# A D-skip by loads and VectorE products in place of diagonal matmuls, with a new instruction order

## The chip, the cores and the metric

The kernel runs on one core of a Trainium2 chip. The metric is the device time of an execution in microseconds (us). A profile covers one execution and gives its span, 1.7 to 2.2 us less than the timed figure in most executions, up to 3.7 us in some. Where a run was timed in rounds, it alternated with the kernel before on the same chip. Executions carry a state: one that is over 1.5% above the fastest of the same kernel counts as slow, and ratios use fast ones only. The trace also gives the clock granted to TensorE, as a share of full speed (1.00 in the profile before).

## The reference, cut to what matters

Two layers side by side, 640 channels each, on a sequence of 2048.

```python
# layer A: a diagonal complex state space layer
for t in range(L):
    h = Lam_bar * h + Bu[:, t, :]
y = 2.0 * einsum("blp,dp->bld", hseq, Cmat).real + x * Dskip   # x * Dskip is the "D-skip"
# layer B: a short shift convolution, a long FFT convolution, and a gate
kv = (k shifted by 0..3, weighted) * v
out_b = q * (longconv(kv, ssm_k) + kv * ssm_D)
```

The change concerns only the last term of layer A. Both layers share the engines all the time.

## The kernel before: the parts that matter

The kernel doesn't leave its order to a scheduler. A long text, `ORDER`, lists about 750 named operations. Each engine executes its own operations in the order of that text, and a suffix says where an operation with a choice goes (`/A` ScalarE, `/D` VectorE, `/G` GpSimd, `/S` SyncE's queue) and which buffer it gets (`@2`).

The names that the argument needs: `dn` are the up-projections of layer A, `m1` a first combination with rotation tables M, `S0` and `S5` the coarse sums over the sequence, `d0`/`a0` and `d1`/`a1` the way back (a matmul, then an addition on VectorE), `py` the output projection in 16 tiles of two halves, `ey` the tile's eviction and `st` its store. `set_4_0` and the like are halves of the tables M (M_4, first five channel groups). `s1`, `s2`, `i2`, `i1` are the stages of layer B's long convolution, `cv`, `cs`, `ca`, `cm` its shift convolution, `kz` a memset of the pad columns of k, `kvl` a reload through DRAM.

The output projection before, with the D-skip as matmuls against blocks of diag(D):

```python
for j in range(10):
    nc.tensor.matmul(P[:, part, 0:320], lhsT=hap(j), rhs=self.CT[:, j, c0:c0 + 320],
                     start=(j == 0), stop=False)
...                                               # pieces: the 2 or 3 blocks of 128 channels in this half
for q, (k, lo, hi) in enumerate(pieces):
    nc.tensor.matmul(P[:, part, lo - c0:hi - c0], lhsT=self.xT[...], rhs=self.diagD[:, k, ...],
                     start=False, stop=(q == len(pieces) - 1))
...
self.evac(f"ey_{r}{i}", 640, ...)                 # a copy on ScalarE or VectorE
```

A table half is one product of two SBUF operands, on either engine:

```python
self.eng[e].tensor_tensor(out=mt[:, js, :]..., in0=E[:]...to_broadcast(...), in1=sap()[:, js, :]...to_broadcast(...), op=ALU.mult)
```

Of the kernel before, what the change touches and what calls it, by code (L numbers as in the profile page):

```python
# [9 lines left out]
ALU = mybir.AluOpType  # L10
# [10 lines left out]
D = 640  # L21
# [125 lines left out]
ld_lre kz2/D@0 w0 xn0@0 scol pidx Dm0 B00 consts J0 w1 E0 kz1/G@1 ci0@1 w2 zero J1 c4 wi1@2 ld_lim ld_ldt xn1@2 wi0@3 bc  # L147
px00@0 B01 px02@1 wm1 nrow ex00/A ex02/A par@2 px04@3 p0 nrowf dtb Dm1/S wm0 B10 px10@0 ex04/A px12@1 E1 px14@2 p1 ex12/A nrho
x121 fi mk rn ph ci1 ld_sk/S dn0_2_0@4 x130 ex10/D trig dn0_0_0@6 B11 ex14/D ws1@4 R dn1_2_0 rc ss dn1_1_0@0 set_3_0/D
set_2_0/G dn1_0_0 e1_2_0/A dn1_4_0@2 set_1_0/D ws0@5 k0@6 kz0/G set_1_1/G x131 dn0_4_0 e1_0_0/D hst0/S@2 m1_2_0 x120 set_3_1/G  # L150
dn0_1_0 e3_2_0/D e1_4_0/D m1_0_0 dn1_8_0@4 ct@3 set_2_1/G e3_0_0/D e1_1_0/D dn0_8_0 sk x101 cv300/D@4 dn1_9_0@6 set_4_1/D
m1_1_0 dn0_9_0 cs200/D@3 v0@5 e1_8_0/A dtap0/D set_8_1/D m1_4_0 e3_1_0/A m1_8_0 e3_4_0/A ca200 s1h03@0,4 x100 e3_8_0/A s1h01@2
e1h03/A dn0_3_0@4 cs100/D x111 e1h01/A ca100 s1h00@0 x110 e1_9_0/A s1h02@2 cs000/D dn1_3_0 kz3/G@2 e1h00/A ca000 hst1/S@6
m1_9_0 e1h02/A dn1_7_0@0 cm00 e1_3_0/A s2h02@2,5 den kvs0/S dn0_7_0 e3_9_0/A k1 e2h02/A set_12_0/D s2h03@6 m1_3_0 g e2h03/A
dn0_4_1@2 e1_7_0/A s2h01@6 dn1_4_1 e2h01/A dtap1/D set_G_0/G set_8_0/D m1_7_0 e3_3_0/A kvl0/S@3 s1h10@6,0 e3_7_0/A k2 s1h12@4
e1h10/A set_G_1/D dn0_0_1@0 set_12_1/G e1h12/A s1h11@6 set_4_0/D dn1_0_1 e1_4_1/A ld_dsk/G e1h11/A m1_4_1 cv310/D@5 s1h13@4
e3_4_1/A cs210/D@4 v1@6 s1k03@6,2 e1h13/A dn0_1_1@2 ca210 e1k03/A s1k00@4 cs110/D e1_0_1/A s1k02@6 V dn1_1_1 e1k00/D e1k02/A
m1_0_1 ca110 e1_1_1/A s2h00@4 s1k01@6 e3_0_1/A cs010/D m1_1_1 e1k01/A dn1_3_1@0 cv320/D@3 e3_1_1/A ca010 s2k03@6,1 e2h00/A
dn0_3_1 cm10 e2k03/A s2k01@2,4 s2k00@4 e2k01/A kvs1/S dn1_2_1@6 e2k00/D k3 e1_3_1/A s2k02@2 pP00@6 s2h11@4,1 e2k02/A dn0_2_1
pQ00 e2h11/A m1_3_1 cn00@3 dn0_8_1@2 e3_3_1/A pP01@5 e1_2_1/A s2h12@4 s2h13@0 pY00 e2h12/A dn1_8_1 e2h13/A m1_2_1 pQ01  # L160
kvl1/S@4 i200@4,4 e3_2_1/A i201@0 e300/A pY01 S0@6 v2@6 e301/A dn1_9_1@4 cs220/D@1 eS0/A ca220 i202@0 e1_8_1/A i203@6 cn10
dn0_9_1 cs120/D e302/A ca120 e303/A s1k10@0,2 m1_8_1 cs020/D e1_9_1/A zt0@5 dn1_6_1@6 e3_8_1/D e1k10/A ca020 m1_9_1 s1k11@2
e3_9_1/A s1k13@0 cm20 e1k11/A s1k12@4 dn0_6_1 e1k13/A e1k12/D jw0@2 e1_6_1/A s2h10@0 q0/S@5 jsw0 dn0_7_1@4 cn11@0 e2h10/A Ct
jcw0 jaw00 scan0 hst2/S@0 s2k13@2,1 s2k12@0 e2k13/A dn1_7_1 e2k12/A dn1_5_0@2 e1_7_1/A s2k11@0,4 pP11@6 cn01 dn0_5_0 e2k11/A
pQ11 m1_7_1 s2k10@0 e3_7_1/A m1_6_1 e2k10/A pY11 dn1_6_0@4 e1_5_0/A i100@0 pP10@1 kvs2/S e3_6_1/A dn0_6_0 dtap2/G ob00 m1_5_0
s1h22@6,4 e3_5_0/A pQ10 e1_6_0/A s1h20@0 dn1_5_1@2 e1h22/A pY10 dn0_5_1 e1h20/A kz4/G@3 k4 diagD hst3/S@4 jv0@6 e1_5_1/A
i213@0,2 jsv0 m1_6_0 e313/A m1_5_1 i211@6 e3_5_1/D e3_6_0/A i212@0 jcv0 e311/A i210@2 kvl2/S@6 jav00 S5@4 v3@1 jav01 e312/A
e310/D d1_0@6 eS5/A ct00@0 a1_0 ct01@2 ect00/A jw5@4 jcw5 s1h23@6 ect01/A dtap3/D jsw5 ct10@0 e1h23/A ct11@2 jaw50 i101@4
scan5 ect11/A ct20@6 ect10/A s1h21@2 ect20/A s1k23@0,1 q1/S@0 ob01 e1h21/A d1_2@6 d1_3@7 a1_2 jv5@4 ob0/S e1k23/A ct21@2 zt1@5
jsv5 ect21/A ct30@0 jcv5 s1k21@4 jav51 ect30/A s1k22@2 jav50 d1_4@6 e1k21/A a1_3 d1_9@0 d1_5@1 a1_4 e1k22/A d1_7@7 a1_9 d1_6@6  # L170
ct31@4 a1_5 ct40@2 ect31/A d1_1@0 a1_6 d1_8@1 a1_7 ect40/A ct41@4 d00_6@6 a1_8 ect41/A d00_7@7 d00_0@2 a1_1 d00_5@3 cs230/A@5
d00_2@1 d00_8@0 a00_5 py0_32@4,0 a00_6 a00_2 py1_32 a00_7 a00_8 s1k20@6 ey_32/A a00_0 d00_9@3 d00_4@1 e1k20/A st_32/S d00_3@0
a00_9 d00_1@2 i111@4 a00_1 cv330/A@6 a00_3 i110@6 a00_4 s1h33@2,0 ca230 py0_03@0,1 e1h33/A ob11 cs130/A py1_03 ob10 py0_33@2,0
ey_03/A ca130 st_03/S ob1/S py1_33 cs030/D ca030 d01_1@4 s1h32@6 ey_33/A a01_1 s1h30@0 st_33/S e1h32/A cm30 d01_9@5 hst4/S@2
d01_3@4 py0_02@2,1 cv340/A@5 cs240/D@1 kvs3/S a01_9 py1_02 e1h30/A ca240 d01_0@5 py0_00@6,0 ey_02/D cs140/A a01_0 st_02/S
dtap4/G s2h20@0,3 a01_3 d01_8@5 s2k21@2,0 e2h20/A a01_8 d01_6@4 py1_00 kvl3/S@6 ca140 e2k21/A a01_6 s2k20@0 ey_00/A d01_5@5
d01_2@4 e2k20/A d02_6@2 st_00/G a01_5 s2h21@6 d01_4@3 a02_6 d01_7@5 e2h21/A py0_31@0,1 a01_7 cs040/A a01_2 s1k33@6,2 a01_4
s1k30@4 s1k32@2 pP20@3 e1k30/A py1_31 e1k32/A ca040 py0_12@4,0 e1k33/A pQ20 q4/S@1 ey_31/A py1_12 pY20 st_31/S d02_5@2 s2h23@6
v4@0 ey_12/A a02_5 d02_3@3 s2h22@0 e2h23/A a02_3 d02_1@2 d02_7@4 d02_2@5 a02_1 e2h22/A s1k31@6 st_12/S a02_2 d02_9@3 e1k31/A
s1h31@0 a02_9 d02_4@2 a02_7 d02_8@5 e1h31/A s2k22@6,6 d02_0@3 a02_8 e2k22/A i220@0,5 a02_4 i221@4 a02_0 e320/A s2h33@6,4 cm40  # L180
s2h30@2 py0_21@0,1 e2h30/A e2h33/D kvs4/S e321/A py1_21 s2k23@2 ey_21/A s2h32@6 e2k23/D st_21/S s1h40@4,1 e2h32/A s1h42@0
kvl4/S@4 pP21@3 s2k31@2,0 e1h42/A py0_20@6,0 e2k31/D e1h40/A s2k32@0,5 pQ21 s2k33@4 e2k32/A s2h31@2 py1_20 pY21 e2k33/A pP31@6
py0_22@0,1 ey_20/A e2h31/A st_20/S pQ31 s1h41@4 s1k40@6,0 pY31 s1h43@2 e1k40/A py1_22 q2/S@2 e1h41/D e1h43/A s2k30@6 ey_22/D
s2h41@2,3 e2k30/A i223@4 st_22/G e2h41/D s1k41@0 e323/A s1k42@6 pP30@5 py0_13@2,0 e1k42/A pQ30 e1k41/A py1_13 pY30 s1k43@4
i222@6 ey_13/D e1k43/A i231@0,2 e322/D st_13/S i232@2 e331/A s2k40@4,4 e332/D s2k41@6 zt2@4 e2k40/A s2h42@0 e2h42/D e2k41/A
s2h40@2 i230@4 e2h40/A i233@6 e330/D py0_30@0,1 e333/A pP40@0 s2h43@2 s2k42@4,3 pQ40 zt3@1 e2h43/A s2k43@6 py1_30 pY40 e2k42/A
e2k43/A py0_23@2,0 ey_30/A pP41@5 i121@4 pQ41 st_30/S q3/S@6 i240@6,0 i241@0 pY41 e340/A py1_23 e341/A i242@6 ey_23/A i243@0
e342/A st_23/G i120@2 e343/D py0_10@6,1 ob20 zt4@5 ob21 i131@0 i130@2 ob31 py1_10 ob30 ob2/S py0_11@4,0 ey_10/D st_10/S ob3/S
py1_11 i140@0 ey_11/A st_11/G i141@2 ob40 py0_01@6,1 ob41 py1_01 ob4/S ey_01/A st_01/S
# [3 lines left out]
class Kernel:  # L193
# [65 lines left out]
    def setup(self):  # L259
# [14 lines left out]


# [24 lines left out]
        Et = T([128, 64], i32, "Et")  # L300

        op("E0", {"POOL": 0.2}, lambda e: g.iota(Et[:], pattern=[[1, 64]], base=128, channel_multiplier=-1), w=["Et"])

        def f_E1():
            v.tensor_single_scalar(out=Et[:], in_=Et[:], scalar=63, op=ALU.bitwise_and)
            v.tensor_single_scalar(out=E[:], in_=Et[:], scalar=0, op=ALU.is_equal)
        small("E1", f_E1, ["Et"], ["E", "Et"], 0.4)
        J = T([128, 128], bf16, "J")
        Jt = T([128, 128], i32, "Jt")
        ident = T([128, 128], bf16, "ident")  # L310
        self.J, self.ident = J, ident
        op("J0", {"POOL": 0.3}, lambda e: g.iota(Jt[:], pattern=[[1, 128]], base=64, channel_multiplier=-1), w=["Jt"])

        def f_J1():
            v.tensor_single_scalar(out=ident[:], in_=Jt[:], scalar=64, op=ALU.is_equal)
            v.tensor_single_scalar(out=Jt[:], in_=Jt[:], scalar=127, op=ALU.bitwise_and)
            v.tensor_single_scalar(out=J[:], in_=Jt[:], scalar=0, op=ALU.is_equal)
        small("J1", f_J1, ["Jt"], ["J", "ident", "Jt"], 1.0)
# [7 lines left out]
        def f_nrow():  # L326
            g.iota(nrow[:, 0:3, :], pattern=[[1, 3], [0, 10]], base=1, channel_multiplier=0)
            g.iota(nrow[:, 3:7, :], pattern=[[4, 4], [0, 10]], base=4, channel_multiplier=0)
        small("nrow", f_nrow, [], ["nrow"], 0.3, "POOL")
        small("nrowf", lambda: v.tensor_copy(out=nrowf[:], in_=nrow[:]), ["nrow"], ["nrowf"], 0.5)  # L330

        lpar = T([128, 3, 10], f32, "lpar")
        lre, lim = lpar[:, 1, :], lpar[:, 2, :]
# [102 lines left out]
        def f_bc():  # L436
# [3 lines left out]
            v.tensor_scalar(out=offc[:], in0=ptmp[:], scalar1=-2048.0, scalar2=4096.0, op0=ALU.mult, op1=ALU.add)  # L440
        small("bc", f_bc, ["pidx"], ["bcol"], 0.6)

        ws = T([128, 96], i32, "ws")
        rowa = T([128, 2], f32, "rowa")
        colw = T([128, 1], f32, "colw")
        pr = T([128, 2], i32, "pr")
# [728 lines left out]
```

## Time and profile before

| | before |
|---|---|
| median of 3 runs | 202.42 us (200.48 to 203.70) |
| profiled span, clock | 200.5 us, 1.00 |
| TensorE busy | 185.7 us, 93% |
| VectorE, ScalarE, GpSimd busy | 168.1, 148.1, 20.6 us |
| first up-projection matmul | 11.93 us |
| first coarse sum S0 | 61.33 to 62.47 us |
| first output projection | 104.6 us |
| last inverse unit (i140) | 191.48 us |

The four marks at the bottom are start times of TensorE's groups in the timeline.

### The profile page before, as it was taken

The page shows a single profiled execution, that of the slowest core. Times are in us where ns is not written, and L with a number is a line of the kernel's source. Part 1 is how long each engine was busy: PE and PEld are TensorE (multiplying, and loading weights), DVE is VectorE, ACT ScalarE, POOL GpSimd, SP SyncE. Part 2 cuts the span into 40 slices and gives each one's busy share as a digit, 9 for nine tenths or more (in the row PEclk, how much of TensorE's full clock was granted, in tenths as well). Part 3 has the DMA queues.
Part 4 walks back from the last instruction along what each step waited for, and adds up shares of the span by engine and source line. Part 5 has one row for each costly group of instructions (what it writes and reads, how often), then busy time and mean ns, then how long its engine had stood idle before and what let it go on. Part 6 is the DMA issues. An engine that isn't in the chain of part 4 may idle for free.

```text
span 200.5 us, 8859 instructions
## 1 busy us (share of the span) xinstructions
PE 185.7 (93%) x4043; PEld 136.3 (68%) x4043; DVE 168.1 (84%) x264; ACT 148.1 (74%) x175; POOL 20.6 (10%) x35
## 2 busy tenths in 40 slices
PE   0599999979999999699999999999999999999982
PEld 0465566747777678467657777676787878788771
DVE  7899899876899999949988899788959999877540
ACT  4979998978899888389986749896967679752011
POOL 8056500700000000000000000100000010001010
PEclk9999999999999999999999999999999999999999
DMA  5999997999999999969995068509334334998985
GB/s 167 239 152 132 231 180 167 245 159 210 219 180 171 167 217 206 247 153 215 210 196 133 5 152 252 134 22 189 89 147 103 96 80 105 170 234 160 229 226 140
DMA packets 109959, 33.74 MB, mean 168 GB/s; under 512 B 107106, under 2 KB 108642, under 8 KB 109922
## 3 DMA queue, kind: packets, MB, share of 16 engines
q1 hardware_dynamic: 109668, 32.52, 83.9%
q8 instruction: 31, 0.51, 1.1%
q0 software_dynamic: 224, 0.66, 0.9%
q14 instruction: 6, 0.05, 0.1%
q10 hardware_dynamic: 30, 0.00, 0.0%
HBM read 9.19 MB, written 7.86 MB: 85 GB/s over the span
## 4 chain that ended last, share of the span: by engine, by line
PE 72%; DMA 14%; DVE 6%; ACT 3%; SPq 2%; issue 1%; POOL 0%; DVEq 0%; POOLq 0%; ACTq 0%
PE ps L806 20%; PE ps L658 17%; PE ps L909 9%; PE ps L945 8%; PE ps L231 4%; DMA s<-s 4%; PE ps L1001 4%; DMA s<-in_B_v_dram 4%; PE ps L233 4%; PE ps L1037 3%; DMA s<-in_A_x_dram 3%; DMA s<-in_B_ssm_k_dram 3%; DVE s L239 2%; PE ps L810 2%; ACT s L237 2%
## 5 line engine op out<-in xcount | busy, mean ns | idle before, releaser
L237 ACT CAST s<-ps 128x1024 bf16<-128x1024 f32 x86 | 84.1, 1018 | 16.9 <-PE ps L945 6.4
L658 PE MATMUL ps<-xT,BC 128*64 128x512 bf16 x400 | 49.1, 383 | 0.1
L806 PE MATMUL ps<-BC,hb 128*128 128x320 bf16 x240 | 36.4, 300 | 0.0
L658 PEld LDWEIGHTS <-BC 128*64 128x64 bf16 x400 | 22.3, 110 | 15.1 <-issue 0.9
L806 PEld LDWEIGHTS <-hb 128*128 128x128 bf16 x240 | 21.9, 98 | 8.7 <-issue 0.3
L968 DVE TENSOR_TENSOR s<-s,s 128x2048 bf16<-128x2048 bf16 x20 | 24.4, 1222 | 2.0 <-ACT s L237 0.7
L909 PE MATMUL ps<-R,s 64*64 64x128 bf16 x1280 | 22.5, 218 | 2.9 <-POOL s L831 1.8
L237 ACT CAST yo<-ps 128x640 bf16<-128x640 f32 x12 | 8.4, 698 | 22.7 <-PE ps L810 18.5
L909 PEld LDWEIGHTS <-s 64*64 64x64 bf16 x1280 | 18.7, 107 | 8.1 <-issue 3.7
L239 DVE CAST s<-ps 128x1024 bf16<-128x1024 f32 x14 | 17.0, 1220 | 8.3 <-PE ps L909 2.7
L945 PE MATMUL ps<-s,Wre 128*64 128x128 bf16 x320 | 21.4, 221 | 0.0
L763 DVE TENSOR_TENSOR hb<-ps,hb 128x512 bf16<-128x512 f32 x30 | 19.1, 684 | 2.8 <-PE ps L231 1.6
L945 PE MATMUL ps<-s,Wim 128*64 128x128 bf16 x320 | 21.2, 219 | 0.0
L945 PEld LDWEIGHTS <-Wre 128*64 128x64 bf16 x320 | 18.2, 110 | 2.5 <-issue 0.5
L884 DVE TENSOR_TENSOR s<-s,s 128x2048 bf16<-128x2048 bf16 x15 | 18.3, 1222 | 1.0 <-ACT s L876 0.7
L945 PEld LDWEIGHTS <-Wim 128*64 128x64 bf16 x320 | 18.1, 110 | 1.1
L1044 DVE TENSOR_TENSOR s<-ps,s 128x1024 bf16<-128x1024 f32 x10 | 11.8, 1216 | 4.1 <-PE ps L1037 3.9
L237 ACT CAST hb<-ps 128x768 bf16<-128x768 f32 x17 | 13.7, 808 | 1.1 <-PE ps L658 1.1
L968 DVE TENSOR_TENSOR s<-s 128x1024 bf16<-128x1024 bf16 x20 | 13.8, 688 | 0.3
L231 PE MATMUL ps<-hb,M 128*64 128x256 bf16 (+1 forms) x136 | 13.3, 296 | 0.0
L1037 PE MATMUL ps<-Ct,s 128*64 128x64 bf16 x640 | 11.6, 196 | 0.8 <-DMA s<-s 0.7
L1037 PEld LDWEIGHTS <-s 128*64 128x64 bf16 x640 | 11.1, 113 | 1.9 <-DMA s<-s 0.9
(157 smaller groups left out, 261.4 us busy)
## 6 DMA issues: line engine op xcount, KB each, us to landing
s<-in_B_ssm_k_dram SPq DMA_DIRECT2D x5, 512.0 KB, 4.7
kvd<-s SPq DMA_DIRECT2D x5, 512.0 KB, 4.4
s<-kvd SPq DMA_DIRECT2D x5, 512.0 KB, 5.6
s<-in_B_q_dram SPq DMA_DIRECT2D x5, 512.0 KB, 4.4
out_dram<-s SPq DMA_DIRECT2D x5, 512.0 KB, 5.1
out_dram<-yo SPq DMA_DIRECT2D x12, 160.0 KB, 2.8
s<-in_A_x_dram SPq DMA_DIRECT2D x2, 640.0 KB, 4.8
out_dram<-yo POOLq DMA_DIRECT2D x4, 160.0 KB, 3.4
```

Of the source, the lines that this page charges most:

```text
L231: self.nc.tensor.matmul(out[h], lhsT=lhsT[:, h], rhs=rhs, **k)
L237: self.nc.scalar.copy(out=out, in_=in_)
L239: self.eng[e].tensor_copy(out=out, in_=in_)
L658: nc.tensor.matmul(P[64 * ri:64 * ri + 64, b, :], lhsT=self.BT[:, k, ri, 64 * j:64 * j + 64], rhs=self.xT[:, k, hf, 2 * b:2 * b + 2, :].re ...
L763: v.tensor_tensor(out=hv(r), in0=self.P(p2)[:, 0, :].rearrange("p (h m) -> p h m", h=2), in1=hv(r), op=ALU.add)
L806: nc.tensor.matmul(P[:, part, 0:320], lhsT=hap(j), rhs=self.CT[:, j, c0:c0 + 320], start=(j == 0), stop=False)
L884: op(f"ca{j}{G}{h}", {"DVE": dve_tt(W_)}, lambda e, c=c, tt=tt: v.tensor_tensor(out=c(), in0=c(), in1=tt(), op=ALU.add), r=[f"tm{G}{h}"], ...
L909: nc.tensor.matmul(P[64 * ri:64 * ri + 64, r, 128 * b4:128 * b4 + 128], lhsT=d[64 * r:64 * r + 64, 4 * qd + b4, a0, :], rhs=self.R[64 * r: ...
L945: nc.tensor.matmul(P[64 * pi:64 * pi + 64, ri, 128 * k4:128 * k4 + 128], lhsT=W[:, kp, pi, :], rhs=A[:, kp + 16 * pi, :], start=True, stop ...
L968: v.tensor_tensor(out=o, in0=a, in1=b, op=op_)
L1037: nc.tensor.matmul(P[64 * ah:64 * ah + 64, b // 8, 64 * (b % 8):64 * (b % 8) + 64], lhsT=Z[:, 16 * h + b, 64 * ri:64 * ri + 64], rhs=self. ...
L1044: v.tensor_tensor(out=o, in0=self.P(pt)[:].rearrange("p s (b a c) -> p a (s b) c", b=8, a=16), in1=o, op=ALU.mult)
```

## The change

The intent is to take 96 small matmuls off TensorE, which is the bound. Each output tile now loads its rows of x again, VectorE multiplies them by D, and the eviction from PSUM becomes an addition. Memory for it is won by letting small buffers share space. B is loaded in three pieces, eight matmuls on zeros run on TensorE as a warm-up, and the whole `ORDER` was searched anew under the assumption that GpSimd and VectorE hold each other up (in the profile before, two table halves that take 1.25 and 0.81 us alone take 1.92 and 1.87 side by side). The code part, cut:

```diff
-                    nc.tensor.matmul(P[:, part, 0:320], ..., start=(j == 0), stop=False)
-                pieces = [...]
-                for q, (k, lo, hi) in enumerate(pieces):
-                    nc.tensor.matmul(P[:, part, lo - c0:hi - c0], lhsT=self.xT[...], rhs=self.diagD[...], start=False, ...)
+                    nc.tensor.matmul(P[:, part, 0:320], ..., start=(j == 0), stop=(j == 9))
-        self.evac(f"ey_{r}{i}", 640, ...)
+        op(f"xl_{r}{i}", ... dma_start(out=self.yo[yo.slot][:], in_=self.x2[r0:r0 + 2033:16, :]) ...)
+        op(f"xm_{r}{i}", ... nc.vector.tensor_tensor(out=yo, in0=yo, in1=self.Db[:], op=ALU.mult) ...)
+        op(f"ey_{r}{i}", ... nc.vector.tensor_tensor(out=yo, in0=self.P(pt)[:, :, 0:320], in1=yo, op=ALU.add) ...)
+        op("warm", {"PE": 1.9}, f_warm, ...)          # eight matmuls on zeros
-        self.yo = [... for i in range(2)]
+        self.yo = [... for i in range(4)]
```

Of the order, one stretch, as the changed kernel has it for GpSimd's queue (other engines' words cut):

```
... kz4/G kz3/G set_4_1/G set_12_0/G set_8_1/G set_12_1/G set_4_0/G set_G_0/G xl_03/G@2 set_8_0/G set_G_1/G xl_02/G@3 ld_dsk/G ... S0
```

Before, GpSimd made six table halves, all by 39 us. VectorE made the other eight.

## The prediction

> **What bounds the kernel now.** I read the page's shares first, then the busy time in stretches, then the chain that ended last, then the idle time of each group, and last the timelines of GpSimd and VectorE around the rotation tables M.
>
> ```profile
> span 200.5 us, 8859 instructions
> PE 185.7 (93%) x4043; PEld 136.3 (68%) x4043; DVE 168.1 (84%) x264; ACT 148.1 (74%) x175; POOL 20.6 (10%) x35
> ...
> 0.00:12.00 12.00, 4.98 (x45) 4.24 (x47) 10.17 (x44) 7.75 (x11) 5.44 (x19) 1.00 0.89 189
> 12.00:42.00 30.00, 30.00 (x520) 18.41 (x522) 27.88 (x54) 28.38 (x38) 12.20 (x10) 1.00 1.06 191
> 42.00:62.00 20.00, 18.89 (x458) 13.90 (x454) 15.98 (x16) 16.57 (x23) 0.00 (x0) 1.00 1.18 188
> 62.00:105.00 43.00, 40.96 (x947) 28.63 (x942) 38.34 (x67) 35.37 (x47) 0.52 (x2) 1.00 1.09 199
> 105.00:191.00 86.00, 85.59 (x1935) 66.74 (x1932) 73.33 (x84) 58.77 (x60) 1.91 (x4) 1.00 0.61 136
> 191.00:200.50 9.50, 5.32 (x154) 4.34 (x154) 2.35 (x2) 1.23 (x2) 0.54 (x1) 1.00 0.72 181
> ```
>
> TensorE is the bound. From 12 to 191 us (columns after the two lengths: TensorE, weight loads, VectorE, ScalarE, GpSimd) it is idle only 1.1 + 2.0 + 0.4 us; the rest of its idle time is the start and the tail. VectorE has about 13 us left between 105 and 191 us. So a microsecond off the matmul stream is a microsecond off the span, and so, reversed, is any new hole in it.
>
> ```profile
> 104.77 1.36 PE ps L806 x10
> 106.13 0.14 PE ps L810 x3
> 106.27 1.36 PE ps L806 x10
> 107.63 0.14 PE ps L810 x3
> ```
>
> This is the chain in the output projection. Each half tile is ten matmuls, 1.36 us, then three against diag(D), 0.14 us.
>
> ```profile
> 9.68 2.31 PE ps L607 x20
> 11.99 8.10 PE ps L658 x35
> ...
> 36.11 1.25 POOL L422 TENSOR_TENSOR M_G<-E,sg 128x640 bf16<-128x640 bf16 x1 [6.34 <-DVE sg L405]
> 37.32 1.92 POOL L422 TENSOR_TENSOR M<-E,ss 128x640 bf16<-128x640 bf16 x1
> ...
> 37.32 0.81 DVE L422 TENSOR_TENSOR M<-E,ss 128x640 bf16<-128x640 bf16 x1
> 38.05 1.87 DVE L422 TENSOR_TENSOR M_G<-E,sg 128x640 bf16<-128x640 bf16 x1
> ```
>
> One table half takes 1.25 us on GpSimd and 0.81 on VectorE alone; where both want one at once, 1.92 and 1.87. All of GpSimd's tables are done by 39.2 us here, more than 20 us before the first coarse sum reads them (61.3 us).
>
> [...] the first 20 transposes of 128 columns take 2.31 us, 116 ns each. [...] the trace has 0.49 and 0.81 us for 640 elements.
>
> **The change, part by part.**
> Removed from TensorE: 6 matmuls in each of 16 tiles, 32 groups x 0.14 = 4.5 us, all in the stream that sets the end, so -4.5 us.
> Added at the start: 8 matmuls of 512 columns on zeros before the second half of x has landed (TensorE waits for it anyway)[...] But the second x load is now issued behind four transposed loads of B where it stood behind one, so I book -0.7 us.
> Moved: the tile eviction goes wholly to VectorE as an addition from PSUM (16 x 0.82 where it had 4, +9.8 us) with a product before it (16 x 0.49 = +7.8). In return VectorE loses 4 evictions of 1024 (-4.9), 2 of 768 (-1.9), 2 table halves, 2 scalings (-1.5), diagD (-1.1), and gains 3 copies of xT (+1.8). With the rows of the page VectorE comes to about 176 us. From the first projection to the last inverse unit (i140) I sum 80 us for it against 78 for TensorE; consecutive VectorE spans overlap by some 0.08 us in the trace, so the real occupancy is lower, and it just fits. I book +0.5 us.
> Loads: 16 x 160 KB are 2.6 MB more on 33.7 MB, mostly when the DMA share is 0.61, far ahead of use: 0.
> Shorter buffers, B in three pieces: 0.
>
> The new order is what I trust least. The semaphores of the built program show one thing plainly. GpSimd's queue is in order, and in it the two small memsets of the pad columns of k for groups 4 and 3 now stand ahead of all eight table halves. The first waits for VectorE's scaling cs120, the second for a matmul of i202 (inverse of group 0), because those buffers are still being read. The first coarse sum on TensorE (S0) waits for the M_4 and M_8 halves, and the seventh of the eight is the one it needs; an x load issued by GpSimd stands among them. So S0 can't start before i202 + about 0.3 + 7 x 1.25 + 0.5 for the load's issue = i202 + 9.6 us with nobody in the way[...]. Between i202 and S0 TensorE has only i203 0.5, one L658 group 1.1, three s1 units 1.5, two of L231 0.66: with i202 itself 4.2 us. All its later work waits behind S0. Before, i202 ran at 63.65 us; the order puts 1.2 us less of matmuls ahead of it, so it comes near 61.5. S0 would be reached near 65.5 and start near 72: a hole of 5 to 9 us, taken as 7. [...]
>
> Sum for the span: 200.5 - 4.5 - 0.7 + 0.5 + 7 + 0.8 = 203.6 us; some later small waits (1.8 us at 82 us, for a load that goes through GpSimd) may dissolve in the hole, -0.9: 202.7. The timed figure stood 1.9 us above the profiled span (202.42 against 200.5), so 204.6 us.
>
> **The rivals.**
> First, no hole: GpSimd's tables finish in time, or TensorE is held before S0 by something that would have come anyway (the kv reload of group 1 lands just about when s1 wants it). Then 200.5 - 4.7 = 195.8, timed 197.7, faster by 2.3%. For it: whoever searched this order must have seen a gain. Against it: the waits are in the program, and nothing in 4.2 us of matmuls covers 9.6 us of GpSimd; a search that counts a buffer's wait only at its first user would miss it, since the k loads now stand ahead of those memsets.
> Second, VectorE becomes the bound after 105 us: 73.3 us busy of 86 before, plus about 8 more of work. If it holds PSUM buffers a little too long for each tile, 16 x 0.2 to 0.3 us make 3 to 5 us more: 207 to 210 timed. For it: the sums above; against: VectorE gains slack during the hole and its products run ahead.
> Third, GpSimd's loads and reloads (kvl2, q1, x tiles) come late[...]: 1 to 2 us at one place. The trace before has only small ones, 3.4 us to landing, against 2.8 from SyncE's queue.
>
> **Range and chances.** Hole of 5 us and everything else good: 199.5 timed. Hole of 9 us with a VectorE-bound second half: 209. Centre 204.5, which is +1%. Faster by over 2% (below 198.4) needs the first rival: 0.14. Slower by over 2% (above 206.5) needs the hole at its long end or the second rival: 0.30. Within: 0.56.
>
> **What would show it.** The matmul groups of L810 gone, TensorE's busy time near 181 us. An idle stretch of TensorE of 5 to 9 us just ahead of the first coarse sum, released by GpSimd's table product, with VectorE and ScalarE idle in it too, and GpSimd's table products at 60 to 73 us instead of 16 to 39. [...] VectorE busy above 90% between 105 us and the end, with its PSUM additions named as what TensorE waits for only in places. I am wrong if the tables run early or TensorE has no such stretch; or if the hole is there but the second half loses more than the first.

## More of the kernel before

The page shows the shape. Each digit is the busy share, in tenths, of one of 40 equal slices of the span (5.0 us each).

```profile
PE   0599999979999999699999999999999999999982
POOL 8056500700000000000000000100000010001010
PEclk9999999999999999999999999999999999999999
```

TensorE is full from the third slice on, the clock row shows no cut, and but for small pieces GpSimd works only in the first 40 us.

## The result, and the profile after

The changed kernel takes 219.70 us in the median of four runs (218.26 to 220.02), against 202.64 us of the kernel before in the same rounds. The ratio is 1.0867, with a 95% interval from 1.0763 to 1.0971: slower. Ratios here are the mean time of one kernel's fast runs over that of the other's in the same rounds, so not quite the ratio of the medians. The prediction was 204.5 us with a range up to 209, so it was wrong.

| mark on TensorE, us | before | after | difference |
|---|---|---|---|
| first up-projection matmul | 11.93 | 15.41 | +3.5 |
| first output projection | 104.61 | 122.47 | +17.9 |
| last inverse unit (i140) | 191.48 | 206.39 | +14.9 |
| end of the span | 200.5 | 217.8 | +17.3 |

All of the loss is there before the first tile is projected, that is, before the first of the new additions. From there to i140 the changed kernel wins 3.0 us back, and in the tail it loses 2.4.

The same three rows of the page as before, now with 5.4 us to a slice:

```profile
PE   0859999999999029999959999999999999999962
POOL 8060000000005992000202000110000000001000
PEclk9967999999999757999996999999999999999999
```

There are three dents in TensorE's row: at the start, in the 14th and 15th slices (71 to 82 us), where GpSimd's row shows 9s, and in the 21st (109 to 114 us). Each is followed by a cut clock (0.50 from 13 to 19, 74 to 84 and 115 to 118 us). The stretches that the prediction cut the kernel before into, read for the changed one (columns after the lengths: TensorE, weight loads, VectorE, ScalarE, GpSimd, then the clock):

```profile
12.00:42.00 30.00, 28.84 (x416) 17.81 (x418) 21.22 (x56) 22.36 (x32) 2.59 (x2) 0.89 0.96 163
62.00:105.00 43.00, 34.20 (x755) 24.09 (x750) 32.10 (x39) 26.57 (x33) 16.38 (x15) 0.88 0.76 152
105.00:191.00 86.00, 83.24 (x1761) 58.26 (x1761) 75.66 (x107) 71.41 (x71) 3.38 (x6) 0.98 0.72 160
```

From 62 to 105 us TensorE idles 8.8 us where it idled 2.0, and its clock is 0.88. Between 105 and 191 us it is nearly full.

**The hole before the first coarse sum.** The timeline of GpSimd in the changed kernel; the columns are start, duration, engine, line, operation, and the bracket is the idle time before the instruction and what ended it:

```profile
67.61 0.19 POOL L845 MEMSET s<- 128x16 bf16 x2 [53.02 <-DVE s L882]
67.77 8.52 POOL L436 TENSOR_TENSOR M<-E,ss 128x640 bf16<-128x640 bf16 x5
```

TensorE's timeline:

```profile
71.00 0.24 PE L233 MATMUL ps<-Qb,ident 128*64 128x128 bf16 x2
76.34 0.32 PE L233 MATMUL ps<-Qb,M 128*64 128x128 bf16 x2 [5.10 <-POOL M L436]
80.35 0.42 PE L233 MATMUL ps<-Qb,M 128*64 128x128 bf16 x4 [3.70 <-POOL M L436]
```

And VectorE's:

```profile
69.70 1.62 DVE L888 TENSOR_TENSOR s<-s,s 128x2048 bf16<-128x2048 bf16 x1
73.02 2.16 DVE L888 TENSOR_TENSOR s<-s,s 128x2048 bf16<-128x2048 bf16 x1
```

GpSimd stood idle for 53 us, held by the two memsets of pads (L845) that wait for VectorE, and then had to make seven tables while the coarse sum waited: 5.10 and 3.70, together 8.8 us. VectorE's additions of 2048 elements take 1.62 and 2.16 us there, where such an addition took 1.22 before:

```profile
65.66 1.22 DVE L884 TENSOR_TENSOR s<-s,s 128x2048 bf16<-128x2048 bf16 x1
```

The two engines hold each other up: GpSimd's five products above take 1.70 us each, its last two, with VectorE idle (79.0 to 81.5 us), 1.27 and 1.26.

**The start.** TensorE again:

```profile
7.10 2.84 PE L340 MATMUL ps<-xT 128*128 128x512 bf16 x8
9.78 0.61 PE L613 MATMUL ps<-ident,s 128*128 128x128 bf16 x8
13.16 2.31 PE L613 MATMUL ps<-ident,s 128*128 128x128 bf16 x20 [2.78 <-DMA s<-in_A_x_dram]
```

The warm-up (L340) runs, and the eight transposes behind it take 0.61 us, 76 ns each, but then TensorE idles 2.78 us for the second x load, and its 20 transposes take 2.31 us, 116 ns each, exactly as long as they did before without a warm-up. The warm-up missed its target. (Before, these 20 took 2.31 us under a clock that reads 1.00, so the clock row doesn't show all of the slow start. In the changed kernel it reads 0.50 from 13 to 19 us.)

**The reload.** The chain that ended last, two of its pieces:

```profile
103.54 10.17 DMA s<-kvd
...
113.75 1.09 PE ps L913 x64
```

The reload kvl2 is issued by GpSimd's queue at 103.5 us and takes 10.17 us to land. Before, SyncE issued it at 90.0 us. TensorE stops 2.0 us for it in the list of waits.

**The tail.** Before, the last tile followed the last inverse unit without a pause. Now:

```profile
210.76 2.88 PE L810 MATMUL ps<-BC,hb 128*128 128x320 bf16 x20 [2.16 <-DVE s L1048]
```

The profile names VectorE here; "What is left" shows why that is doubtful.

### The profile page after: what moved, and what is told of

It is laid out like the page before. It is cut to its first block, busy times and chain, and to the rows that moved or that the text cites. A ratio compares the mean times of both kernels' runs of the same rounds, so it can differ in the third digit from the quotient of the medians.

```text
span 217.8 us, 8685 instructions
## 1 busy us (share of the span) xinstructions
PE 191.0 (88%) x3951; PEld 131.6 (60%) x3951; DVE 173.9 (80%) x281; ACT 147.8 (68%) x168; POOL 29.7 (14%) x44
## 4 chain that ended last, share of the span: by engine, by line
PE 65%; DMA 12%; DVE 8%; POOL 5%; ACT 3%; SPq 3%; issue 2%; POOLq 0%; ACTq 0%
PE ps L662 19%; PE ps L810 16%; PE ps L913 9%; PE ps L949 8%; DVE s L972 5%; DMA s<-kvd 5%; DMA s<-s 4%; POOL M L436 4%; PE ps L233 4%; PE ps L235 4%; ACT s L239 3%; DMA s<-in_A_x_dram 3%; PE ps L1041 2%; SPq L639 2%; PE ps L1005 2%
## 5 line engine op out<-in xcount | busy, mean ns | idle before, releaser
L239 ACT CAST s<-ps 128x1024 bf16<-128x1024 f32 x90 | 87.4, 1018 | 21.1 <-PE ps L949 6.6
L662 PE MATMUL ps<-xT,BC 128*64 128x512 bf16 x400 | 50.5, 397 | 0.0
L972 DVE TENSOR_TENSOR s<-s,s 128x2048 bf16<-128x2048 bf16 x20 | 24.5, 1223 | 3.1 <-ACT s L239 1.5
L913 PE MATMUL ps<-R,s 64*64 64x128 bf16 x1280 | 23.9, 220 | 2.8 <-DMA s<-kvd 2.0
L888 DVE TENSOR_TENSOR s<-s,s 128x2048 bf16<-128x2048 bf16 x15 | 19.6, 1309 | 0.2
L239 ACT CAST hb<-ps 128x768 bf16<-128x768 f32 x19 | 15.0, 803 | 5.8 <-PE ps L662 5.6
L949 PEld LDWEIGHTS <-Wim 128*64 128x64 bf16 x320 | 17.9, 110 | 1.0
L818 DVE TENSOR_TENSOR yo<-ps,yo 128x640 bf16<-128x640 f32 x16 | 13.2, 822 | 5.6 <-PE ps L810 4.4
L880 ACT ACTIVATE s<-s,sk 128x2048 bf16<-128x2048 bf16 x8 | 15.9, 2003 | 1.1 <-DVE s L888 0.8
L233 PEld LDWEIGHTS <-M 128*64 128x64 bf16 x166 | 9.1, 121 | 11.8 <-POOL M L436 9.1
L823 POOL DMA_DIRECT2D out_dram<-yo x6 | 3.3, 551 | 81.2 <-DVE yo L818 81.2
L241 DVE CAST s<-ps 128x1024 bf16<-128x1024 f32 x10 | 12.1, 1223 | 2.2 <-PE ps L913 0.8
```

The lines of the kernel that those rows point to most:

```text
L233: self.nc.tensor.matmul(out[h], lhsT=lhsT[:, h], rhs=rhs, **k)
L239: self.nc.scalar.copy(out=out, in_=in_)
L241: self.eng[e].tensor_copy(out=out, in_=in_)
L662: nc.tensor.matmul(P[64 * ri:64 * ri + 64, b, :], lhsT=self.BT[:, k, ri, 64 * j:64 * j + 64], rhs=self.xT[:, k, hf, 2 * b:2 * b + 2, :].re ...
L818: op(f"ey_{r}{i}", {"DVE": dve_p(640)}, lambda e: nc.vector.tensor_tensor(out=self.yo[yo.slot][:].rearrange("p (b n) -> p b n", b=2), in0= ...
L880: nc.scalar.activation(out=out, in_=k(j), func=ACT.Copy, scale=self.sk[:, G, j:j + 1])
```

## The experiments

The first theory, T1, after reading the traces: the order cost the time, through three separate faults (pads ahead of the tables in GpSimd's queue; x behind B; reloads on GpSimd), and the new D-skip itself is sound. The rival, T2: VectorE's product and addition are the loss. A later one, T3: wherever GpSimd's tables are put, they and VectorE's operations stretch each other, and that is the loss of the first half.

### Repairing the order, one fault at a time

**e1_pads.** The two pad memsets go behind the tables in GpSimd's queue.

```diff
- kz4/G kz3/G set_4_1/G set_12_0/G ... set_8_0/G set_G_1/G
+ set_4_1/G set_12_0/G ... set_8_0/G set_G_1/G kz4/G kz3/G
```

> The changed kernel with one move in GpSimd's queue: the two memsets of the pad columns of k (groups 4 and 3) stand behind the eight table halves instead of ahead of them. Theory of the hole: the first coarse sum then finds its tables ready; the 8.8 us of TensorE idle at 71 to 80 us and the half-rate stretch after it go, about 10 us: 219.7 becomes 208 to 211. Rival, VectorE is the bound: [...] the time only falls to 215 to 219.

Measured: 217.87 us in the median, but only one execution (211.08) counts as fast, so there is no ratio. The median meets the rival's figure (215 to 219), the one fast execution just about the theory's (208 to 211). The hole at S0 is gone. In its place GpSimd's tables now run from 17 us on, and VectorE's timeline there reads (the small chain den, g, on 10 columns):

```profile
17.64 1.23 DVE L400 TENSOR_TENSOR den<-lpar 128x10 f32<-128x10 f32 x1
18.98 1.11 DVE L402 TENSOR_TENSOR den<-den,t 128x10 f32<-128x10 f32 x1
21.34 1.19 DVE L409 SCALAR_TENSOR_TENSOR g<-cs,ga 128x10 f32<-128x10 f32 x1
```

The same operations took 0.16 to 0.17 us in the kernels before and after. About every second one of the chain is stretched, to 0.93 to 1.23 us, the better part of one GpSimd product; those between stay at 0.15 to 0.22. (The profile fell on an execution labelled slow; in e4_three's, a fast one, the three take 1.22, 1.11 and 1.19 us.) The operations of 0.16 us that take up to 1.23 here run beside GpSimd's products of 1.36 us each (five in 6.78 us from 16.95 us on). The tables that VectorE makes behind this chain come late, and TensorE waits 2.8 us for the first of them at 24 us. The hole had moved and become a chain of small waits. S0 starts at 73.8 us.

**e2_x_early.** The second x load is issued right behind the first piece of B.

```diff
- xn0@0 ... B00 ... B10 ... B01 ... B11 ... xn1@1
+ xn0@0 ... B00 xn1@1 ... B10 ... B01 ... B11
```

> The changed kernel with only the second load of x issued right behind the first transposed load of B, as in the kernel before, not behind four. Theory: the first up-projection starts near 12 us in place of 15.4 and, since TensorE does not pause 2.8 us after the warm-up matmuls, runs at 0.216 us a pair in place of 0.266: 4 to 5.5 us less, 214 to 216. Rival: what follows waits for VectorE or a transfer anyway and the start is given back ahead of the coarse sum: 218 to 220.

Measured: 218.95 us median (214.96 to 220.86), ratio 1.0653, interval 1.0469 to 1.0836. By its two fast runs of four about 2% better than the changed kernel, as expected, but the spread is as large as the gain, the intervals overlap, and the medians differ by 0.8 us only.

**e3_reload_sp.** The reload kvl2 and the load q1 go to SyncE.

```diff
- kvl2/G@1 ... q1/G@0
+ kvl2/S@1 ... q1/S@0
```

> The changed kernel with only the kv reload of group 2 and the q load of group 1 issued from SyncE's queue again, not GpSimd's. Theory: the reload took 10.2 us from issue to landing from GpSimd's queue, against 4.7 to 5.6 for the others; TensorE's stop of 2.0 us at 111.7 us and the half-rate stretch after it go: 2.5 to 4 us less, 216 to 217. Rival: the reload is slow because the DMA engines are full then (share 1.06), whichever queue issues it: 219 to 220.

Measured: 218.86 us median (214.83 to 221.41), ratio 1.0631, interval 1.0460 to 1.0801. Two fast runs of four. Again about 2% by the fast runs, as expected, with the same reserves.

**e4_three.** All three repairs.

> All three of these repairs together in the changed kernel. Theory, three independent losses of the order: 10 + 5 + 3 us come back, 219.7 becomes 201 to 203, close to the kernel before (202.6) or a little below, because the 4.5 us of diagonal matmuls are gone. Rival, VectorE is the bound of the second half: not below 206.

Measured: 211.76 us median, ratio 1.0392 (1.0239 to 1.0544). The three give back half the loss, not all of it, and 201 to 203 was missed. The stop for the reload is gone. TensorE is busy only 6.56 of the 10 us from 20 to 30 us, waiting 3.4 us for a table of VectorE, and the first projection starts at 113.2 us, 8.6 us later than before. T1 in its simple form fell: something else in the first half costs as much as the pads did.

### Does the new D-skip itself cost time?

**e5_order.** The order of the kernel before, with the new D-skip put into it (and the shared small buffers that make room for it), nothing else: `diagD` out, `xl`, `xm` in, all `ey` on VectorE, no warm-up, B in four transposes.

```diff
- py0_32@4,0 ... ey_32/A st_32/S
+ xl_32/S@0 ... xm_32 ... py0_32@4 ... ey_32 st_32/S
```

> The D-skip alone: the order of the kernel before (no warm-up matmuls, B in four transposes, first half untouched) with the new loads, products and additions put into it, all 16 evacuations of the output on VectorE. If the order is what cost the time and the new D-skip is sound: 4.5 us less TensorE work (96 matmuls) and some of it lost to VectorE, 198 to 201 us, and no hole before the first coarse sum, which starts at 60 to 62 us as before. Rival, that the product and the addition on VectorE are themselves the loss (21 us more of VectorE work in the second half): 206 us or more, with TensorE waiting for VectorE between 110 and 190 us.

Measured: 210.72 us median, ratio 1.0360 (1.0287 to 1.0432). T1's 198 to 201 missed; T2's figure was met. The first half is as before (first projection at 104.8 us); the loss lies where T2 puts it. A piece of its chain:

```profile
126.49 0.82 DVE yo L817
127.32 0.40 DVE yo L815
127.71 1.83 DVE hb L766 x3
129.55 1.13 DVE s L887
```

The chain runs through VectorE: addition of the tile, product of the next, and only then the `a0` additions (L766) that later matmuls need.

**e5_order_b.** The same with seven evictions and one scaling moved from VectorE to ScalarE.

> The same, with seven evacuations and one scaling of the second half moved from VectorE to ScalarE, which no longer evacuates the outputs: if VectorE's load limits the first version this one is 1 to 3 us faster, 197 to 199 us; if the order is all, both are the same within 1 us.

Measured: ratio 1.0438 (1.0332 to 1.0544), two fast runs of six, not faster. Handing over work without finding a new order for it doesn't help; I can't say more from it.

**e6_no_diag.** The kernel before without its 96 matmuls. Its output is wrong, which doesn't matter for the time.

```diff
-                    ..., start=(j == 0), stop=False)
-                for q, (k, lo, hi) in enumerate(pieces): ...
+                    ..., start=(j == 0), stop=(j == 9))
```

> The kernel before without its 96 diagonal matmuls (the result is wrong on purpose, the skip term is missing): if TensorE sets the end throughout the second half, the 4.5 us of these matmuls come off in full, 197.5 to 198.5 us. Rival, that another engine or the loads stand right behind TensorE there: 200 to 202 us. This is the most that any other D-skip can gain in this order.

Measured: 200.48 us median, ratio 0.9843 (0.9771 to 0.9916), so 3.2 us of 203.8. The median lies in the rival's range, the mean of the fast runs (199.8) between the two: most of the 4.5 us comes off, not all. This is the most that any other D-skip could win in this order.

**e10_no_product.** e5_order without the 16 products (wrong).

```diff
- xm_32 xm_03 ...  and the operation xm
```

> The version with the D-skip alone in the order of before, without its 16 products x times D (7.7 us of VectorE; the result is wrong on purpose). If VectorE's work is what made that version 7 us slower than before: 4 to 7 us faster than it, 203 to 206 us. Rival, that the waits come from the loads of x, the buffers or the place of the additions: less than 2 us faster, 208.5 us or more.

Measured: ratio 1.0136 (1.0067 to 1.0204), 206.61 us median. That is 2.2% below e5_order, some 4.5 us for 7.7 us of products, as expected if VectorE is the bound.

**e13_evac_dve.** e6_no_diag with all 16 evictions on VectorE, no loads, no products (wrong).

```diff
- ey_32/A ey_03/A ...
+ ey_32/D ey_03/D ...
```

> The kernel before without its diagonal matmuls and with all 16 output evacuations on VectorE in place of four; no loads, no products, no additions (the result is wrong on purpose). It divides the 6 us between the version without the diagonal matmuls (200.5) and the one with loads and additions but without products (206.6): if it is the place of the evacuation on VectorE, 204 to 207 us; if it is the loads of x, 200 to 202 us.

Measured: ratio 1.0079 (1.0033 to 1.0125), 204.37 us median. So the ladder is, in ratios to before: no D-skip 0.9843; all evictions on VectorE 1.0079; with loads and additions 1.0136; with products 1.0360. Times 203 us, the steps are 4.8, 1.2 and 4.5 us. The middle one, the loads with additions in place of copies, lies within the intervals of its two runs. So removing the matmuls was worth 3.2 us, and doing their work on VectorE cost 10.5 us in this order. The stretches show why (columns as above; first the version without any D-skip, then e5_order):

```profile
105.00:170.00 65.00, 64.94 (x1455) 48.46 (x1453) 60.57 (x71) 52.34 (x53) 1.37 (x3) 1.00 0.52 124
105.00:170.00 65.00, 58.38 (x1213) 41.93 (x1212) 60.51 (x81) 41.38 (x37) 1.36 (x3) 0.97 0.54 137
```

VectorE is busy 93% of these 65 us in both. It was nearly full already, so more work for it only pushes TensorE (64.94 to 58.38) and ScalarE aside.

### Can the good halves be joined?

**e8_graft.** The order of before up to its first projection, from there the changed order with the new D-skip; buffers given out anew.

> A graft: the order of the kernel before up to its first projection, and from there the changed kernel's order with the new D-skip (buffers given out anew, the two late reloads issued by SyncE, no warm-up matmuls, B in four transposes). If the loss of the changed kernel lies in its first half alone and its second half holds the D-skip without loss: first projection at 104 to 106 us as before, then the 95 us that the changed kernel takes from there, less the 2 us stop for the reload: 198 to 201 us. Rival, that the new D-skip cannot be held beside the rest of the second half by any of these orders: 205 us or more, as in the version with the D-skip alone.

Measured: 217.18 us median, ratio 1.0614 (1.0537 to 1.0691). Missed. TensorE is busy only 5.55 us of 110 to 120, just behind the seam.

**e9_graft_s5.** The same, cut at the second coarse sum.

> The same graft, cut earlier, at the second coarse sum. If only the part before the first coarse sum is bad in the changed order: within 2 us of the other graft, 198 to 202 us. If the stretch from the second coarse sum to the first projection loses too (19.6 us in the changed kernel, 14.2 before): about 4 us slower than the other graft.

Measured: 219.83 us median, ratio 1.0779 (1.0691 to 1.0866). TensorE waits 8.2 us at the seam for VectorE. The operations that one order had done early and the other late pile up there, so both grafts measure the seam. They tell nothing of the second half.

### The first half: GpSimd's tables

**e7_den_late.** e4_three with VectorE's small chain (den, g) put behind the tables it makes first, where the kernel before has it.

```diff
- ss set_1_0/D ... den ... g ... set_3_0/D ... set_2_1/D
+ ss set_1_0/D ... set_3_0/D ... set_2_1/D den g
```

> The three repairs together, and the small chain of VectorE (den, g and what follows) put behind the tables it makes for the first half, where the kernel before has it. If the loss of the three-repair version at 17 to 30 us comes from these small operations being stretched by GpSimd's tables (1.1 us in place of 0.16) and so from late tables for TensorE: the chain is short again, TensorE is full from 20 to 30 us (over 9 of 10 us busy) and the time falls by 3 to 4 us to 207 to 209. Rival, that the first half waits for the B transposes and x anyway: no change, 211 to 212.

Measured: 215.47 us median, ratio 1.0521 (1.0407 to 1.0635). No gain. The first part of the expectation came true: TensorE is full from 20 to 30 us and the chain's operations take 0.16 us again. But the tables of GpSimd that depend on the chain moved with it. GpSimd's timeline:

```profile
32.00 1.35 POOL L435 TENSOR_TENSOR M_G<-E,sg 128x640 bf16<-128x640 bf16 x1 [8.49 <-DVE sg L418]
```

VectorE's:

```profile
33.55 3.91 DVE L887 TENSOR_TENSOR s<-s,s 128x2048 bf16<-128x2048 bf16 x1
```

TensorE's:

```profile
37.66 1.92 PE L912 MATMUL ps<-R,s 64*64 64x128 bf16 x64 [6.00 <-DVE s L834]
```

One addition of 1.22 us now takes 3.91, and TensorE waits 6.00 us for what follows it on VectorE. The hole moved a third time. That is T3's pattern: late, early or in between, the tables on GpSimd cost in this order. It isn't a rule: in the kernel before, GpSimd made six halves from 16.6 to 39.2 us, two of VectorE's took 2.63 us together in place of 1.55, and TensorE was busy all of the 30.00 us from 12 to 42.

**e11_tables_dve.** e7_den_late with all eight tables given to VectorE (0.82 us each), spread over 38 to 90 us. No arithmetic on GpSimd is left between 17 us and 66 us.

```diff
- set_4_1/G set_12_0/G set_8_1/G set_12_1/G set_4_0/G set_G_0/G set_8_0/G set_G_1/G
+ ... e2h00/D set_12_0/D ... dtap1/D set_8_0/D ... e1_0_1/D set_4_0/D ... e302/D set_4_1/D ... cm20 set_8_1/D ...
```

> The three-repair version with the small chain put late, and now all eight table halves that GpSimd made given to VectorE (0.82 us each, three before the first coarse sum, three before the second, two after): no GpSimd arithmetic is left between 17 us and the end. [...] no operation of VectorE there is stretched (additions 1.22 us, products of tables 0.82), TensorE is full from 20 to 60 us, the first projection starts at 106 to 109 us in place of 113 and the time is 204 to 207. Rival, that the changed order's first half waits for the late x and B and for VectorE's own chain: 210 us or more.

Measured: 206.25 us median, ratio 1.0177 (1.0125 to 1.0229), in all three points as T3 expected. Its VectorE timeline:

```profile
17.00 2.30 DVE L435 TENSOR_TENSOR M<-E,ss 128x640 bf16<-128x640 bf16 x3
29.65 0.16 DVE L400 TENSOR_TENSOR den<-lpar 128x10 f32<-128x10 f32 x1
32.42 1.22 DVE L887 TENSOR_TENSOR s<-s,s 128x2048 bf16<-128x2048 bf16 x1
```

TensorE's timeline at the wait that took 6.00 us in e7_den_late:

```profile
33.83 1.09 PE L912 MATMUL ps<-R,s 64*64 64x128 bf16 x64 [0.68 <-DVE s L834]
```

Nothing is stretched: three tables in 2.30 us, 0.16 us, 1.22 us. The first projection starts at 108.2 us in place of 113.1, and TensorE is busy 38.3 of the 40 us from 20 to 60 (33.4 in e7_den_late). Giving VectorE 6.6 us more work made the kernel 3.3% faster, by the two ratios. The edit changes two things at once, the engine and the place of the tables; tables left on GpSimd but spread in the same way weren't tried.

**e15_only_tables.** The changed kernel with this one edit alone; pads, x, reloads and warm-up stay as they are.

> The changed kernel as it is (pads, x loads, reloads, warm-up and the small chain where it has them), with one edit: the eight table halves that GpSimd made late are made by VectorE, as in the repaired version that reached 206.3. If the placement of these tables on GpSimd, whether late (hole before the first coarse sum) or early (VectorE stretched), is the main cause: the first coarse sum starts at 64 to 66 us in place of 71 to 80, no wait of TensorE for GpSimd's tables, 208 to 211 us against 219.7. Rival, that pads, x and reloads matter as much: 213 or more.

Measured: one fast execution of 205.15 us; the other five are slow, four of 210.57 to 215.70 us (clock 0.967 to 0.989) and one of 241.74 us at a clock of 0.76 (0.75 in every 10 us from 20 us on), on which the profile fell. There is no ratio. The median, 213.09 us, meets the rival's figure (213 or more). What can be said for the theory: its fastest execution is 13.1 us below the fastest of the changed kernel (218.26), below the 208 that was expected, and no slower than e11_tables_dve's (205.44). The start of S0 can't be read from a profile at that clock. So at its best this one edit is worth what all four were together, but one execution is thin evidence for the exact share.

### What is left

**e12_start.** e11_tables_dve without the warm-up and with the third parameter load earlier.

```diff
- xn0@0 ... ld_ldt B00 xn1@1 ... ld_lim ... wz/D ... warm@2
+ xn0@0 ... ld_ldt ld_lim B00 xn1@1 ...
```

> The same, without the eight warm-up matmuls and with the third parameter load moved up. If the warm-up and that load hold up the first transposes: the first up-projection matmul about 2 us earlier and the time 1.5 to 2.5 us below the run beside it. Rival, [...] same within 1 us.

Measured: 210.41 us median, ratio 1.0277 (1.0199 to 1.0355), two fast runs. The first up-projection matmul is at 11.80 us, 3.0 us earlier and where it was before, and yet the kernel isn't faster: first projection at 109.4 us.

**e17_sk_early.** e12_start with the small load for the key scalings moved ahead.

> The repaired version with no warm-up (first up-projection matmul at 11.8 us as before, but no faster in the end) and the small load for the key scalings moved ahead of the other B transposes. VectorE idled 3.6 us for that load and then came to the matrix that the first filter transforms read. If this wait is where the early start was lost: first projection at 105 to 107 us and 203 to 205 us. Rival: no change, 206 to 210.

Measured: 207.65 us median, ratio 1.0182 (1.0096 to 1.0267), no different from e11_tables_dve; its first projection is at 109.4 us too. (Its profile is of an execution labelled slow.) The rival expectation held: the early start is lost again before the first projection, and not in the wait for this load. In part the record shows where: up to the first projection TensorE stops 2.22 us at 34 us for VectorE in e12_start (0.68 in e11_tables_dve) and 2.5 us with no wait named (1.7). The rest stays open.

**e16_no_product.** e11_tables_dve without the products (wrong).

> The repaired version (all tables on VectorE) without its 16 products x times D (the result is wrong on purpose). In the order of before the products cost 4.1 us. If the changed order's second half, with the scalings of the keys on ScalarE, holds the new D-skip: 205 to 206 us against 206.3, under 1 us. Rival, that VectorE is the bound there too: 202 to 203.5 us.

Measured: 208.21 us median, ratio 1.0275 (1.0196 to 1.0353). No gain at all from 7.7 us less of VectorE, where in the order of before it gave 4.5. In the changed order these products don't bind. VectorE's stretch in e11_tables_dve:

```profile
108.00:170.00 62.00, 61.17 (x1332) 44.58 (x1332) 56.42 (x74) 52.23 (x48) 1.92 (x4) 1.00 0.69 155
```

VectorE is at 91%, TensorE at 99%, and ScalarE has taken the scalings of the keys: 52.23 of 62 us, against 41.38 of 65 in e5_order.

**e14_hybrid.** The kernel before with the new D-skip for its last five tiles only, where VectorE has room.

```diff
- py0_30 (with diagD) ... ey_30/A
+ xl_30/S xm_30 py0_30 ... ey_30        (likewise 23, 10, 11, 01)
```

> The kernel before with the new D-skip for its last five output tiles only, where VectorE has room (7.5 and 5.8 of 10 us busy from 170 to 190 us in the version without the diagonal matmuls), the diagonal matmuls staying for the other eleven. 30 of 96 matmuls go, 1 to 1.4 us; if VectorE's free time there carries the rest: 201.5 to 202.5 against some 203 of before, faster by under 1%. If even there the addition costs: 203 to 205.

Measured: 208.50 us median, ratio 1.0192 (1.0119 to 1.0265). Missed, slower even there.

No correct version beat the kernel before; the best, e11_tables_dve and e17_sk_early, stay 1.8% behind. From the first projection to the end of the span, e11_tables_dve takes 203.0 - 108.2 = 94.8 us, before 200.5 - 104.6 = 95.9, and the version without any D-skip 196.8 - 103.8 = 93.0. So even in its best surroundings the new D-skip won about 1 us of the 2.9 to be had there, and 3.6 us are lost ahead of it. These are single profiles, and e11_tables_dve's fast spans alone range from 203.0 to 203.9, so the 1 us isn't clear of the spread.

**A loss that no experiment aimed at.** In most of the new versions TensorE also stops where the profile names no wait ("issue"): 6.9 us in all in e4_three, 5.5 in e12_start, 6.3 in e17_sk_early, 2.2 in e11_tables_dve, 2.0 in e7_den_late, 0.5 in the changed kernel, none in the kernel before. In e4_three, e7_den_late, e11_tables_dve, e12_start and e17_sk_early the first three stand at like places, at 52 to 58, 74 to 81 and 148 to 154 us, each ahead of matmuls of L912; in e4_three, e12_start and e17_sk_early a fourth stands before the last matmuls of the output. TensorE's timeline in e12_start:

```profile
196.49 1.26 PE L809 MATMUL ps<-BC,hb 128*128 128x320 bf16 x8
199.40 1.79 PE L809 MATMUL ps<-BC,hb 128*128 128x320 bf16 x12 [1.65 <-issue]
```

This stop stands 12 matmuls before the end of TensorE's work. The 2.16 us pause ahead of the last tile in the changed kernel stands 20 before the end, and so does the fourth stop of e4_three (3.32 us, named "issue"); both have the eight matmuls of the warm-up, which e12_start hasn't, so all three follow the same number of matmuls, 3931. So the count places the tail's pause, not the data, and it most likely belongs to this family and not to VectorE. Counted with the pause at this place, e11_tables_dve has 3.65 us of such stops (2.19 and 1.46), more than the 2.5 us by which its span exceeds the one before. With one profile for each version it isn't known whether they go with the order or with the execution, and none was removed by a run. They also blur comparisons: e4_three has 3.3 us more of them than e11_tables_dve, e7_den_late only 0.4, so of these two comparisons with e11_tables_dve only that of e7_den_late is nearly free of them.

## Why the prediction was wrong, point by point

It missed by 15.2 us (219.7 against 204.5). The step that failed is the sum for the first half, up to the first projection: -0.7 for the start, +7 for the hole, +0.8 for slow matmuls behind it, -0.9 for waits that dissolve, +6.2 us in all, where 17.9 were measured. (Past it, -4.0 were expected, from -4.5 and +0.5, and -0.6 measured.) The hole itself was right. Most of the error is in TensorE's own work around it: the prediction wanted TensorE "near 181 us" busy and measured is 191.0. With the spans (202.7 predicted, 217.8 measured), 10.0 of the 15.1 us missing in the span are busy time and 5.1 idle time (26.8 us where 21.7 follow from the prediction).

- *"so -4.5 us"* for the removed matmuls: 3.2 us, by e6_no_diag. Right in kind, 1.3 us too large (e6_no_diag's profile holds an "issue" stop of 1.13 us that the kernel before doesn't have).
- *"I book -0.7 us"* for the start, the author's estimate: the first up-projection matmul came 3.5 us later. Wrong in sign. The prediction itself named the second x load behind four loads of B and didn't follow it to the clock: TensorE idled 2.78 us between warm-up and transposes. By i202, expected near 61.5 us, it was 66.66. The warm-up itself took 2.84 us of TensorE. (The 20 transposes that the prediction calls the first are the second 20; of the first, 16 took 1.89 us at 4.98 us, 118 ns each, so the figure holds for both.) Whether the start cost 3.5 us at the end isn't shown; in the repaired order an earlier start brought nothing.
- *"I book +0.5 us"* for VectorE in the second half: not contradicted in the changed order (e16_no_product gained nothing; VectorE was 88% busy from 105 to 191 us, not above 90%). The second rival, VectorE as the bound, was wrong here, and right in the order of before (e5_order).
- *"a hole of 5 to 9 us, taken as 7"*: right in place and cause, at the long end: 8.8 us, from GpSimd's tables behind the pads, at 71 us. (VectorE, expected idle in it, was busy until 77.7 us; i202 and the hole came some 5 us later than forecast.)
- *"+ 0.8"* for slow matmuls behind the hole, the author's estimate: the term that was mis-sized most. The clock was at half (0.50) after each of three stops, not one. An estimate from the trace (TensorE's busy time multiplied by one minus the granted clock, in windows of 1 us) gives 3.1 us after the start, 2.1 after the hole and 1.7 after the reload, 6.8 in all; before, none. The groups of S0 show the half rate directly: they follow each other every 0.43 us after the hole, every 0.22 before.
- *"some later small waits ... may dissolve in the hole, -0.9"*: the wait that it names did go (1.76 us at 84 us before, none now). But a new stop of 2.0 us for the reload came. The third rival had it, at 1 to 2 us; it wasn't in the sum.
- Not in the prediction: the tail, 2.4 us more from i140 to the end, of which 2.16 are the pause before the last tile.

TensorE's two times close the account. Busy: 185.7 before, less 4.5 of matmuls by the prediction's reading, plus 2.8 of warm-up and some 6.8 of slow clock, makes 190.8; measured 191.0. Idle rose by 12.0: the hole 8.8, the reload 2.0, the pause before the last tile 2.2, the start 1.3 and "issue" stops 0.5, less 2.9 of two waits that went; 0.1 is left. That is an account of one profile each, not a set of separate measurements.

The deeper miss is one of reading. The prediction put the hole down to the pads ahead in GpSimd's queue. Moving the pads (e1_pads) removed the hole, and by the medians (217.87 against 219.70) most of the time was lost elsewhere; the one fast execution is 7.2 us below the changed kernel's fastest. The prediction had seen that two products of 0.81 and 1.25 us become 1.87 and 1.92 together, and had used that for the hole's length only. For the repaired versions the experiments show this mutual stretching to be the main thing (7 us or 3.3% between e7_den_late and e11_tables_dve); for the changed kernel itself that rests on e15_only_tables' one fast execution. Eight halves on GpSimd are by estimate 10 us of its time (8 times 1.25), and they cost wherever TensorE was waiting for them or for VectorE's in-order chain: at 70 us as a hole, at 17 us as small operations stretched about sevenfold, at 33 us as one addition of 3.91 us. The chances (0.30 for slower) were too low accordingly.

## What to carry to other kernels

Work moved to GpSimd to spare VectorE is not free here: a table half of 0.81 us on VectorE took 1.87 beside one on GpSimd, which took 1.92 in place of 1.25. Price it by what it adds to VectorE's whole chain, look at the smallest operations there, since they suffered most (0.16 us became 0.93 to 1.23), and ask whether the bound engine waits for that chain at that time. When a hole is repaired, look at once for where the same work now stands; a hole that moves three times points to the work, not to its place. After a stop of TensorE count the slow matmuls behind it: here, behind three stops, they cost by estimate 6.8 us, almost as much as the hole (8.8). And ask of an exchange between engines how full the receiver is in just that stretch: taking 3 us from a full TensorE for 17 us on a VectorE at 93% (12 more evictions at 0.82 us, 16 products at 0.48) is a loss in that order, before any detail.
